# Where a batch's attention groups are cut into the matmul stream: two groups moved from one unit to the next

## The chip, the core and the metric

The kernel runs on one core of a Trainium2 chip. The metric is device time in microseconds (us) of one execution; the median of five runs is given. TensorE (PE) does the matmuls and its weight loads, VectorE (DVE) and ScalarE (ACT) move results out of the accumulation banks (PSUM) and do the elementwise work, GpSimd (POOL) and SyncE (SP) issue the transfers.

## What is computed

Linformer attention followed by a maxout layer. For each of 8 batches and 8 heads, with 1024 positions and head size 64:

```
k_proj = E @ k ;  v_proj = F @ v                  # 64 x 64 per head
attn   = softmax(q @ k_proj^T / 8)                # 1024 x 64
x      = attn @ v_proj                            # heads side by side: 8192 x 512
out    = max(x @ w1, x @ w2) @ w_out              # 512 -> 1024 -> 512
```

The kernel writes max(a, b) as relu(a - b) + b, so it needs x @ (w1 - w2) with a relu, and the product w2 @ w_out once.

## The kernel before

The main work is cut into 16 **units**, two for each batch: unit n handles one half of the positions of batch n // 2. A unit has a "down" part (the layer's second product, line 632, stored to the output) and an "up" part (the first product, line 554). Both are written as seven products in place of eight (a Strassen-like scheme), so there are sums of blocks on DVE (`step_s`, line 515), copies of partial results on ACT (`keep`, line 525) and adds on DVE (lines 569 and 656).

The order of the instructions is written by hand as a list of **slots**. Each down product of a unit is cut into pieces: two pieces of six matmuls in unit 0, three pieces of four in the others. A piece has the key `("P", unit, product, piece)`. In units 1 to 14 the up products of the next unit stand between the pieces, seven in each half, with keys `("U", unit, half, product)`; and in each half there is one empty slot `("G", unit, half)`. `at_slot(key, step, ...)` hangs further work behind a slot. All engines take their instructions in this order; each waits by semaphores for what it needs.

Attention of a batch consists of:

- `step_kv` (line 172): project k and v (16 matmuls of 512 columns into one bank), copied out by ACT (line 191) and DVE (lines 196, 200).
- the transposes: of the projected k (`step_kpt`, 16 small matmuls, or a transposing transfer on SP from batch 3 on), and of q (`step_qt`, matmuls copied out by DVE at line 242, for batches 0 and 1; `step_qt_dma`, two transposing transfers on SP, from batch 2 on).
- four **groups** (g, j): g picks four of the eight heads, j one half of the positions. A group has 16 score matmuls (line 266), exponentials on ACT, 8 matmuls for the sums (line 278), a logarithm and an exponential on ACT that invert them, 16 matmuls for the values (line 278 too), and products on DVE that write x (`xt_sb`). Unit 2n needs the two groups with j = 0 of batch n, unit 2n + 1 those with j = 1.

These small matmuls use a quarter or an eighth of the array each, and several run beside each other.

There are two forms of a group. The **loose** form (`step_sc`, `step_dn`, `step_inv`, `step_at`) hangs scores, sums, inversion and values at slots of their own. Its scores go to a pair of attention banks (`att_banks`, two pairs in turn as they come free), its values to two ordinary banks (`mm_bank`), and DVE multiplies each with a product of its own (line 325, two instructions of 512 columns). The **merged** form (`step_group`) puts the scores of one group and the sums and values of the group before it into one G slot; scores go to two ordinary banks with one exponential for each (line 351), sums and values to the two pairs of attention banks, the inversion is at lines 370 and 373, and one DVE product of 1024 columns (line 377) is issued at slot U 2 by `step_later`. In the batch's first group the scores stand behind the sums and values of the old group, in the others ahead of them.

Before the change, all four groups of batch 1 are in the loose form and hang at the pieces of unit 0, and the merged form begins with batch 2 in unit 1: its first scores at the second G slot. Batch 2's projection hangs at the first G slot of unit 1.

Transfers: POOL issues the loads of k, v and q (1 MB each). Batch 2's v and q are issued behind batch 1's projection. SP issues the stores of the output (256 KB each) and the transposing transfers in program order. The loads of batch 3 hang at `("U", 1, 0, 6)` behind `step_gate`, a POOL copy that waits for batch 2's transposed q.

Of the kernel before, what the change touches and what calls it, by code (L numbers as in the profile page):

```python
# [16 lines left out]
def kernel(  # L17
# [14 lines left out]
    B, H, S, D = q.shape  # L32
# [27 lines left out]
    def mm_bank(dtype=FP32, n=None):  # L60
        if n is None:
            n = turn.pop(0)
            turn.append(n)
        return ps.tile([128, 512 if dtype == FP32 else 1024], dtype, tag=f"mm{n}", name="mm_ps")

    def att_banks(dtype=FP32):
        return ps.tile(
            [128, 2, 512 if dtype == FP32 else 1024], dtype, tag="att", bufs=2, name="att_ps"
        )
# [6 lines left out]
            name=nc.get_next_instruction_name(),  # L76
# [30 lines left out]
    tiles = {b: {} for b in range(B)}  # L107
# [180 lines left out]
    def values_into(t, g, j, at_ps):  # L288
        for z in range(2):
            tiles_into(  # L290
                lambda o: at_ps[o][:, z * W : (z + 1) * W], t["ex", g, j],
                lambda rows, hh: t["vp"][rows, 4 * g + hh, z, :],
            )

    def new_xt(t):
        t["xt"] = xpool.tile([128, NP2, 2, HALF], FP16, tag="xt", name="xt_sb")

    def x_out(t, g, j):
        return t["xt"][:, 2 * g : 2 * g + 2, :, j * W : (j + 1) * W]
# [15 lines left out]
        ld = t["ld", g, j]  # L315
        nc.scalar.activation(out=ld, in_=ld, func=ACTF.Exp, scale=-1.0)

    def step_at(t, g, j):
        if "xt" not in t:
            new_xt(t)  # L320
        ld = t.pop(("ld", g, j))
        at_ps = [mm_bank() for _ in range(2)]
        values_into(t, g, j, at_ps)
        for o in range(2):
            nc.vector.tensor_tensor(  # L325
                out=x_out(t, g, j)[:, :, o, :],
                in0=at_ps[o].rearrange("q (z n) -> q z n", z=2),
                in1=ld[:, o, None, :].broadcast_to([128, 2, W]),
                op=ALU.mult,
            )  # L330
# [121 lines left out]
    U = {(b, o): {"n": n, "b": b, "o": o, "t": tiles[b]} for n, (b, o) in enumerate(units)}  # L452
# [260 lines left out]
    t = tiles[0]  # L713
# [25 lines left out]
    step_dn(t, 1, 0)  # L739
    step_inv(t, 1, 0)  # L740
    step_at(t, 0, 0)
    step_dn(t, 1, 1)
    step_inv(t, 0, 1)
    step_kv(t, 4, 8, "v")
    step_inv(t, 1, 1)
    step_at(t, 1, 0)
    step_wd(0)

# [7 lines left out]
    def loads(b, *names):  # L756
# [4 lines left out]

    slots = [
        (0, u0[0]), (None, f(step_at, 0, 1)), (1, u0[1]), (None, f(step_at, 1, 1)),
        (None, lambda: loads(1, "v", "q", "k")),
        (None, wd[1]), (2, u1[0]), (3, u1[1]), (4, u0[2]), (None, wt[0]), (5, u0[3]),
# [31 lines left out]
    def at_slot(key, s, *a):  # L797
        steps.setdefault(key, []).append(lambda: s(*a))
# [11 lines left out]
    t = tiles[1]  # L810
    at_slot((0, 19), new_attn, t)
    at_slot((0, 19), lambda: turn.__setitem__(slice(None), [2, 3]))
    for n, x in enumerate((
        "kv", "", "kpt", "qt00 qt10", "", "sc00 qt01 qt11", "sc10", "dn00 in00", "sc01",
        "at00 dn10 in10", "sc11", "at10 dn01 in01", "dn11 in11", "at01", "at11",
    )):
        key = ("P", 0, (n - 1) // 2, (n - 1) % 2) if n else (0, 19)
        for name in x.split():
            if name[0] == "k":
                if name == "kpt":  # L820
                    at_slot(key, step_kpt, t, 0, H, True)
                else:
                    at_slot(key, step_kv, t)
                    at_slot(key, loads, 2, "v", "q")
            else:
                g, j = int(name[2]), int(name[3])
                s_ = {"qt": step_qt, "sc": step_sc,
                      "dn": step_dn, "in": step_inv, "at": step_at}[name[:2]]
                at_slot(key, s_, t, *((4 * g, 4, 2 * j, 2 * j + 2) if name[:2] == "qt" else (g, j)))
        if n in (1, 5):  # L830
            at_slot(key, step_t, 1, (0, 1) if n == 1 else (2, 3))
        if 6 <= n < 10:
            at_slot(key, sums_x, U[0, 1], ((2, 0, 1, 3)[n - 6],))


    t = tiles[2]
    at_slot(("P", 0, 6, 0), new_attn, t)
    at_slot(("G", 1, 0), step_kv, t, 0, H, "kv", True)
    at_slot(("U", 1, 0, 1), step_kpt, t, 0, H, True)
    at_slot(("G", 1, 0), step_qt_dma, t, 0, H // 2)  # L840
    at_slot(("G", 1, 0), step_qt_dma, t, H // 2, H)
    at_slot(("U", 1, 0, 6), step_gate, t, "qt")
# [2 lines left out]
    for b in range(3, B):  # L845
        t = tiles[b]
        n = 2 * b - 3
# [3 lines left out]
        at_slot(("U", n, 0, 1), step_kv, t, 0, H, "kv", True, True)  # L851
        at_slot(("U", n, 0, 6), step_gate, t)
        at_slot(("U", n, 0, 6), loads, b + 1, "k", "v", "q")
    groups = [(tiles[b], g, j) for b in range(2, B) for j in range(2) for g in range(2)]
    none = (None, None, None)
    for i, (new, old) in enumerate(zip([*groups, none], [none, *groups])):
        n, h = divmod(i + 3, 2)
        if new[0] is not None:
            at_slot(("G", n, h), lambda t=new[0], h=h: t.__setitem__("first", (h, 1 - h)))
        at_slot(("G", n, h), step_group, *new, *old)  # L860
        at_slot(("U", n, h, 0), step_later)
        at_slot(("U", n, h, 2), step_later)
# [59 lines left out]
```

The softmax here doesn't subtract the row's maximum and nothing guards it: scores larger than these inputs give would overflow.

## Time and profile before

| | |
|---|---|
| median of 5 runs | 334.15 us (333.97 to 334.52) |
| the profiled execution | 333.97 us |
| its span, first to last instruction | 332.2 us |
| mean granted TensorE clock | 0.993 |
| PE busy | 320.1 us, 96% |
| DVE busy | 240.0 us, 72% |
| ACT busy | 201.6 us, 61% |
| chain that ended last | PE 86%, DMA 6%, DVE 4% |
| unit 0's pieces | 54.5 to about 71.5 us |
| unit 1's pieces and up products | about 71.5 to 91 us |

A matmul's record starts when it starts and its end is modelled, so records overlap; how long a stretch of matmuls really holds PE is read from the start of one to the start of the next that follows it. Busy shares are means over the whole span.

### The profile page before, as it was taken

The page shows a single profiled execution, that of the slowest core. Times are in us where ns is not written, and L with a number is a line of the kernel's source. Part 1 is how long each engine was busy: PE and PEld are TensorE (multiplying, and loading weights), DVE is VectorE, ACT ScalarE, POOL GpSimd, SP SyncE. Part 2 cuts the span into 40 slices and gives each one's busy share as a digit, 9 for nine tenths or more (in the row PEclk, how much of TensorE's full clock was granted, in tenths as well). Part 3 has the DMA queues.
Part 4 walks back from the last instruction along what each step waited for, and adds up shares of the span by engine and source line. Part 5 has one row for each costly group of instructions (what it writes and reads, how often), then busy time and mean ns, then how long its engine had stood idle before and what let it go on. Part 6 is the DMA issues. An engine that isn't in the chain of part 4 may idle for free.

```text
span 332.2 us, 9012 instructions
## 1 busy us (share of the span) xinstructions
PE 320.1 (96%) x3852; PEld 247.9 (75%) x3852; DVE 240.0 (72%) x426; ACT 201.6 (61%) x358; POOL 37.1 (11%) x56
## 2 busy tenths in 40 slices
PE   7976999999999999999999999999999999999994
PEld 3542546658788788878888788878887888888883
DVE  1345598997686779677969879677967796969572
ACT  1462522655677677767777577777776777764541
POOL 8546002003000030003000020003000000000000
PEclk9997999999999999999999999999999999999999
DMA  7999999997995969995999899997999321212132
GB/s 150 202 199 170 207 207 204 197 197 159 192 232 129 196 93 207 223 193 100 192 241 201 131 143 230 205 191 96 217 210 185 88 96 34 97 34 95 35 127 96
DMA packets 74680, 53.14 MB, mean 160 GB/s; under 512 B 29456, under 2 KB 74512, under 8 KB 74640
## 3 DMA queue, kind: packets, MB, share of 16 engines
q0 software_dynamic: 29376, 28.31, 54.3%
q1 hardware_dynamic: 45264, 24.25, 30.3%
q8 instruction: 30, 0.49, 0.6%
q14 instruction: 10, 0.08, 0.1%
HBM read 57.15 MB, written 16.78 MB: 223 GB/s over the span
## 4 chain that ended last, share of the span: by engine, by line
PE 86%; DMA 6%; DVE 4%; issue 1%; POOL 1%; ACT 1%; DVEq 0%; POOLq 0%
PE mm_ps L632 43%; PE mm_ps L554 25%; PE mm_ps L400 5%; PE att_ps L180 3%; DMA big<-in_moe_w_dram 3%; PE att_ps L278 3%; PE mm_ps L266 3%; DMA k_sb<-in_k_dram 3%; PE mm_ps L436 2%; DVE xt_sb L325 1%; DVE o_sb L656 1%; DVE gt_sb L569 1%; POOL k_sb L102 1%; PE mm_ps L237 1%; PE mm_ps L180 1%
## 5 line engine op out<-in xcount | busy, mean ns | idle before, releaser
L525 ACT COPY p_sb<-mm_ps 128x512 f32<-128x512 f32 x172 | 97.2, 593 | 46.8 <-PE mm_ps L554 33.2
L632 PEld LDWEIGHTS <-big 128*128 128x128 f16 x768 | 73.4, 98 | 12.3 <-issue 3.7
L632 PE MATMUL mm_ps<-T_sb,big 128*128 128x256 f16 x576 | 78.1, 273 | 0.0
L569 DVE TENSOR_TENSOR gt_sb<-mm_ps,p_sb 128x512 f16<-128x512 f32 x56 | 38.5, 688 | 46.5 <-PE mm_ps L554 46.5
L554 PE MATMUL mm_ps<-big,big 128*128 128x256 f16 x336 | 50.4, 273 | 0.0
L554 PEld LDWEIGHTS <-big 128*128 128x128 f16 x448 | 43.8, 98 | 5.2
L632 PEld LDWEIGHTS <-gt_sb 128*128 128x128 f16 x384 | 35.6, 98 | 10.1 <-issue 5.8
L632 PE MATMUL mm_ps<-wo_sb,gt_sb 128*128 128x256 f16 x256 | 42.9, 273 | 0.1
L554 PEld LDWEIGHTS <-wd_sb 128*128 128x128 f16 x336 | 32.9, 98 | 4.1 <-issue 0.3
L554 PE MATMUL mm_ps<-xt_sb,wd_sb 128*128 128x256 f16 x224 | 33.6, 273 | 0.2 <-ACT ex_sb L351 0.2
L351 ACT ACTIVATE ex_sb<-mm_ps 128x512 f16<-128x512 f32 x48 | 26.1, 596 | 9.2 <-PE att_ps L278 7.0
L656 DVE TENSOR_TENSOR o_sb<-mm_ps,p_sb 128x512 f32<-128x512 f32 x32 | 21.9, 685 | 10.7 <-PE mm_ps L632 7.2
L377 DVE TENSOR_TENSOR xt_sb<-att_ps,ld_sb 128x1024 f16<-128x1024 f32 x24 | 29.2, 1219 | 0.1
L632 PE MATMUL mm_ps<-m_sb,xt_sb 128*128 128x256 f16 x128 | 24.4, 273 | 0.0
L604 ACT ACTIVATE gt_sb<-mm_ps 128x512 f16<-128x512 f32 x28 | 16.8, 600 | 8.7 <-PE mm_ps L554 8.7
L515 DVE TENSOR_TENSOR big<-gt_sb 128x1024 f16<-128x1024 f16 x32 | 21.9, 684 | 0.2
L572 DVE TENSOR_SCALAR gt_sb<-gt_sb 128x512 f16<-128x512 f16 (+1 forms) x56 | 20.4, 364 | 1.9
L632 PE MATMUL mm_ps<-wo_sb,big 128*128 128x256 f16 x128 | 21.5, 273 | 0.0
L632 PE MATMUL mm_ps<-T_sb,gt_sb 128*128 128x256 f16 x128 | 21.5, 273 | 0.0
L632 PEld LDWEIGHTS <-xt_sb 128*128 128x128 f16 x192 | 18.8, 98 | 2.2
L229 POOL COPY junk<-kpt_sb 1x1 f16<-1x1 f16 x5 | 0.9, 178 | 166.4 <-DMA kpt_sb<-kp_sb 166.4
L400 PE MATMUL mm_ps<-xt_sb,wd_sb 128*128 128x512 f16 x64 | 16.3, 400 | 3.0 <-DVE wd_sb L414 2.1
(86 smaller groups left out, 435.4 us busy)
## 6 DMA issues: line engine op xcount, KB each, us to landing
out_dram<-o_sb SPq DMA_DIRECT2D x63, 256.0 KB, 2.7
k_sb<-in_k_dram POOLq DMA_DIRECT2D x7, 1024.0 KB, 10.6
v_sb<-in_v_dram POOLq DMA_DIRECT2D x7, 1024.0 KB, 17.3
q_sb<-in_q_dram POOLq DMA_DIRECT2D x7, 1024.0 KB, 22.3
k_sb<-in_k_dram POOLq DMA_DIRECT2D x4, 256.0 KB, 7.1
q_sb<-in_q_dram POOLq DMA_DIRECT2D x4, 256.0 KB, 8.3
v_sb<-in_v_dram POOLq DMA_DIRECT2D x2, 512.0 KB, 12.9
big<-in_moe_w_dram POOLq DMA_DIRECT2D x8, 128.0 KB, 10.7
```

Of the source, the lines that this page charges most:

```text
L180: nc.tensor.matmul(out=kv_ps[r * KP : (r + 1) * KP, 0:n], lhsT=eft[:, i, c, :], rhs=t[w][:, h0:h1, c, :], start=(c == 0), stop=(c == NC - 1),)
L351: nc.scalar.activation(out=t["ex", g, j][:, e, :], in_=banks[e], func=ACTF.Exp, scale=scale)
L377: nc.vector.tensor_tensor(out=x_out(t, g, j).rearrange("q z o n -> q o z n"), in0=at_ps.rearrange("q o (z n) -> q o z n", z=2), in1=ld[:, ...
L400: nc.tensor.matmul(out=h_ps, lhsT=wd_sb[:, r, fb * 128 : (fb + 1) * 128], rhs=t["xt"][:, r, :, j * W : (j + 1) * W], start=(r == 0), stop= ...
L515: nc.vector.tensor_tensor(out=S(i), in0=x, in1=y, op=op)
L525: copy(out=x, in_=bank)
L554: nc.tensor.matmul(out=bank[:, m * W : (m + 1) * W], lhsT=w_[:, n_, (2 * d + m) * 128 : (2 * d + m + 1) * 128], rhs=a[:, n_, :], start=(n ...
L569: nc.vector.tensor_tensor(out=c_blk(j, c), in0=two(x), in1=two(y), op=ALU.add)
L572: nc.vector.tensor_scalar_max(ap, ap, 0.0)
L604: nc.scalar.activation(out=out, in_=in_, func=ACTF.Relu)
L632: nc.tensor.matmul(out=bank[:, i * CH : (i + 1) * CH], lhsT=a(c)[:, i * 128 : (i + 1) * 128], rhs=w_(c), start=(n is not None and m == (lo ...
L656: nc.vector.tensor_tensor(out=o_sb, in0=two(x), in1=two(y), op=ALU.add)
```

## The change

Two of batch 1's four groups stay in unit 0, in the loose form, but gathered into three spots: both scores; both sums with their inversions; then the values of both together with the scores of the third group. The values of the second group go to a pair of attention banks (new argument `att` of `step_at`). The transposes of q for the second half of the positions get two slots of their own. The sums and values of the third group, and the whole fourth group, become merged groups at the two G slots of unit 1. So the list `groups` begins two groups earlier, and the pairs of new and old group are shifted. From unit 2 on the order is the same as before. Batch 2's projection goes from the first G slot of unit 1 to slot U 1 of that half, and its k transposes from U 1 to U 4.

```diff
-    def step_at(t, g, j):
+    def step_at(t, g, j, att=False):
         if "xt" not in t:
             new_xt(t)
         ld = t.pop(("ld", g, j))
-        at_ps = [mm_bank() for _ in range(2)]
+        if att:
+            both = att_banks()
+            at_ps = [both[:, o, :] for o in range(2)]
+        else:
+            at_ps = [mm_bank() for _ in range(2)]
         values_into(t, g, j, at_ps)
...
     for n, x in enumerate((
-        "kv", "", "kpt", "qt00 qt10", "", "sc00 qt01 qt11", "sc10", "dn00 in00", "sc01",
-        "at00 dn10 in10", "sc11", "at10 dn01 in01", "dn11 in11", "at01", "at11",
+        "kv", "", "kpt", "qt00 qt10", "", "sc00 sc10", "qt01", "qt11", "",
+        "dn00 in00 dn10 in10", "", "", "at00 AT10 sc01", "", "",
     )):
...
                 s_ = {"qt": step_qt, "sc": step_sc,
-                      "dn": step_dn, "in": step_inv, "at": step_at}[name[:2]]
-                at_slot(key, s_, t, *((4 * g, 4, 2 * j, 2 * j + 2) if name[:2] == "qt" else (g, j)))
+                      "dn": step_dn, "in": step_inv, "at": step_at, "AT": step_at}[name[:2]]
+                args = (4 * g, 4, 2 * j, 2 * j + 2) if name[:2] == "qt" else (g, j)
+                at_slot(key, s_, t, *args, *([True] if name[:2] == "AT" else []))
...
     t = tiles[2]
     at_slot(("P", 0, 6, 0), new_attn, t)
-    at_slot(("G", 1, 0), step_kv, t, 0, H, "kv", True)
-    at_slot(("U", 1, 0, 1), step_kpt, t, 0, H, True)
+    at_slot(("U", 1, 0, 1), step_kv, t, 0, H, "kv", True)
+    at_slot(("U", 1, 0, 4), step_kpt, t, 0, H, True)
     at_slot(("G", 1, 0), step_qt_dma, t, 0, H // 2)
     at_slot(("G", 1, 0), step_qt_dma, t, H // 2, H)
...
-    groups = [(tiles[b], g, j) for b in range(2, B) for j in range(2) for g in range(2)]
+    groups = [(tiles[b], g, j) for b in range(1, B) for j in range(2) for g in range(2)][2:]
     none = (None, None, None)
-    for i, (new, old) in enumerate(zip([*groups, none], [none, *groups])):
-        n, h = divmod(i + 3, 2)
+    for i, (new, old) in enumerate(zip([*groups[1:], none], groups)):
+        n, h = divmod(i + 2, 2)
```

## The prediction

> **What bounds the kernel now.** I read the page's busy lines and slices first, then PE's waits in the stretch that the change touches, then PE's timeline there, then the DVE, ACT and SP timelines beside it.
>
> ```profile
> PE 320.1 (96%) x3852; PEld 247.9 (75%) x3852; DVE 240.0 (72%) x426; ACT 201.6 (61%) x358; POOL 37.1 (11%) x56
> ...
> PE 7976999999999999999999999999999999999994
> ...
> PEclk9997999999999999999999999999999999999999
> ```
>
> From slice 6 (49.8 us) on PE is never under 90% busy, so from there time falls only if PE gets less to do or loses a gap. The waits view of PE between 52 and 110 us has two rows:
>
> ```profile
> PE mm_ps L278 <- DVE xt_sb L325: 0.6, 2, 0.3
> PE mm_ps L554 <- ACT ex_sb L351: 0.2, 1, 0.2
> ```
>
> That is little, but "busy" hides a second cost. The timeline of PE (start, duration, engine, line, tiles, count):
>
> ```profile
> 60.58 0.82 PE L632 MATMUL mm_ps<-T_sb,big 128*128 128x256 f16 x6
> 61.33 0.41 PE L266 MATMUL att_ps<-qt_sb,kpt_sb 64*32 64x256 f16 x16
> 61.67 0.83 PE L632 MATMUL mm_ps<-T_sb,big 128*128 128x256 f16 x6
> 62.43 0.30 PE L278 MATMUL att_ps<-ex_sb,ones 64*32 64x256 f16 x8
> 62.66 0.83 PE L632 MATMUL mm_ps<-T_sb,big 128*128 128x256 f16 x6
> ...
> 69.45 0.61 PE L632 MATMUL mm_ps<-T_sb,gt_sb 128*128 128x256 f16 x4
> 69.90 0.38 PE L632 MATMUL mm_ps<-T_sb,xt_sb 128*128 128x256 f16 x2
> 70.59 0.27 PE L278 MATMUL mm_ps<-ex_sb,vp_sb 64*32 64x256 f16 x1 [0.31 <-DVE xt_sb L325]
> 71.19 0.41 PE L278 MATMUL mm_ps<-ex_sb,vp_sb 64*32 64x256 f16 x15 [0.33 <-DVE xt_sb L325]
> 71.53 0.61 PE L632 MATMUL mm_ps<-wo_sb,gt_sb 128*128 128x256 f16 x4
> ```
>
> ```profile
> 82.37 1.04 PE L632 MATMUL mm_ps<-T_sb,big 128*128 128x256 f16 x8
> 83.33 0.41 PE L266 MATMUL mm_ps<-qt_sb,kpt_sb 64*32 64x256 f16 x16
> 83.68 0.61 PE L632 MATMUL mm_ps<-T_sb,big 128*128 128x256 f16 x4
> 84.47 0.60 PE L554 MATMUL mm_ps<-xt_sb,wd_sb 128*128 128x256 f16 x4 [0.18 <-ACT ex_sb L351]
> ...
> 90.79 0.38 PE L632 MATMUL mm_ps<-wo_sb,gt_sb 128*128 128x256 f16 x2
> 91.11 0.41 PE L266 MATMUL mm_ps<-qt_sb,kpt_sb 64*32 64x256 f16 x16
> 91.33 0.29 PE L278 MATMUL att_ps<-ex_sb,ones 64*32 64x256 f16 x8
> 91.44 0.40 PE L278 MATMUL att_ps<-ex_sb,vp_sb 64*32 64x256 f16 x16
> 91.78 0.39 PE L632 MATMUL mm_ps<-wo_sb,gt_sb 128*128 128x256 f16 x2
> ```
>
> Read starts, not durations. Six 128*128 matmuls take 0.66 (54.50 to 55.16, between two pieces with nothing between). From 60.58 to 61.67 is 1.09, so sixteen score matmuls in a spot of their own cost 0.43. Inside the merged spot at 91.11 the same sixteen take 0.22, eight sums 0.11, and the whole spot (scores, sums, values) 0.99 - 0.22 for its two big matmuls = **0.77**, where alone they would be 0.43 + 0.33 + 0.44 = 1.20. So each change from big to small matmuls and back costs about 0.21, whatever stands in the spot.
>
> **What the change moves, and its price on PE.** Work stays; spots go from eleven to five. Before, each spot by start differences less 0.66: scores 0.52 (58.49 to 59.67), 0.43, 0.48, 0.47; sums 0.33, 0.34; values and sums together 0.55 twice; values 0.44; the last values 1.42 (69.45 to 71.53). Sum 5.53. The last one holds a stall of 0.98: its two banks come free only as the two products L325 at 69.86 and 70.46 end, queued on DVE behind two adds L656 and six other L325. The eleventh spot, scores of batch 2 at 83.33, costs 1.31 - 0.87 = 0.44, and the next up product then waits for its bank's exponential: 84.47 instead of 84.12, 0.35. Total before: 5.53 + 0.44 + 0.35 = **6.32**.
>
> After, in order:
> - Both first scores in one spot: 0.52 + 0.22. The second needs the second transposed half of q, which DVE (L242, a pair that starts at 58.59 and ends at 59.87) has ready for PE at about 59.93, while PE arrives at 59.55: a new wait of 0.38. Queued behind it on PE is everything. Together **1.12**.
> - Both sums: 0.33 + 0.11 = **0.44**. Their exponentials (1.0 each on ACT) end near 61.8, PE comes near 63.9: hidden.
> - Values, values into an attention bank, scores: 0.44 + 0.22 + 0.22 = **0.88**. The banks' last readers are the two transposed copies and the two logarithms L312, all done by 66.0, PE comes at 66.3; the margin is thinnest here (0.3) for the second logarithm, which only the scores need, 0.4 later.
> - The first spot of unit 1, scores, sums, values: 0.77. Its values use the bank that the four products L325 read. These run behind two adds: PE's seventh product ends near 66.2, adds from 66.40, products from 67.60 at 0.60 each, the last over at 70.10. PE wants the bank at about 70.12, the release needs some 0.05: **0.81**. If DVE is late, PE pays one for one.
> - The second spot of unit 1 is a batch's first, where sums and values go ahead of the scores. The like spot in unit 3 (117.13 to 118.99, eight big matmuls out) takes 0.99, not 0.77. One piece later the up product waits for the exponential as it did before, 0.35: **1.34**.
>
> Total after: 1.12 + 0.44 + 0.88 + 0.81 + 1.34 = **4.59**. Difference 1.73.
>
> What else moves: the transposes of q are split over two slots; 128*128 transposes next to big matmuls cost no change (56.28 to 56.95 is 0.67 for six matmuls), so nothing. Batch 2's projection costs 72.20 to 74.80 less 0.66 = 1.94; in unit 3 it stands in the new slot and costs 110.37 to 112.75 less 0.44 = 1.94: nothing. Its k transposes cost 0.46 in either slot; they need the ACT copy L191 and the release of the projection's bank by DVE L196 (near 76.6 by DVE's rows from 75.3 on), PE comes at 77.7. The four L325 of 0.60 become two L377 of 1.22 on DVE, and two exponentials of 1.0 become four of 0.54: off PE's path while DVE has its gaps (15.14 busy of 20.24 between 71.60 and 91.84); without that cover 2.4 at most.
>
> SP keeps its order: four stores, then batch 2's two transposing transfers. They wait for q's landing (issued 55.73, 15.6 later, 71.3) and not for PE, and their first half lands 5.3 after issue, near 76.8; scores need it near 81.2. POOL's next loads hang on the second half, as before. Batch 3's q must land before 107.82 - 1.73 = 106.1; it landed at 103.1. Unit 2 and on have the same order as before, with PE full (35.85 per two units), so what is won by 85 us is kept to the end.
>
> **The rule that speaks against it.** Stores leave about 2 us earlier, while q is still coming in. The answer on the tiles of those transfers: that q took 15.6 from issue to landing, the one store that shared the time with it
>
> ```profile
> DMA to landing us min/median/max: 7.2/7.2/7.2
> ```
>
> where the next three took 2.7 to 4.0. Three stores of 256 KB at 205 GB/s (that stretch) are 3.8: q lands between 71.3 and 75.1, its first half by 80.5, in time by 0.7; batch 3's q by 106.9 at the latest, 0.8 late. I take nothing for it, and 0.8 as the far end. The Trainium skill, page "DMA: Bandwidth & Descriptors", section "Issuing engines are not separate DMA queues", says that transfers of all issuing engines share 16 DMA engines and interleave. By that rule alone the whole 3.8 would fall on q, the far end above; by the row of the three stores nothing would.
>
> **Sum.** The profiled execution took 333.97 with a span of 332.20; the median of the runs is 334.15. 333.97 - 1.73 = 332.24; with the 0.18 between profile and median, **332.4**. 0.2%, about what a measurement of this kernel can tell from no change, is 0.67.
>
> **Rivals.**
> - *The waits eat less.* Without the waits of 0.38, 0.35 and 0.22 it would be 331.45, the low end. Against: each has a row. Inside the forecast's own range.
> - *The transfers collide* (above), 0.8 to 1.2 lost in unit 3: 333.2 to 333.6. For: DMA engines are full until 70 us. Against: slack of 3.0 (106.1 - 103.1) for q and 0.5 for batch 3's transposed k (landed 117.90, scores 118.43).
> - *The saving does not come.* The 0.21 per spot could be a wait in disguise that reappears elsewhere: 333.5 to 334.8, no change. Against: it is equal in spots with different neighbours (0.33 and 0.34, 0.55 and 0.55).
> - *DVE becomes the bound in unit 1*, on the slower side: two L377 (2 x 1.22) and the projection's L196 and L200 (0.69 + 0.29) all stand in front of L569, which frees the bank of batch 2's scores. Uncovered they cost 3.42 - 1.73 = 1.7 above the median: 335.8. It decides from the point where L569 is over 1.2 late. Against: units 2 and on carry the same rows with DVE at 14 of 17.9 and PE full.
>
> **Chances.** Forecast (331.4 to 333.0) 0.75; collision 0.10; no saving 0.09; DVE bound 0.06. Range **331.4 to 333.5**: the forecast and nearly all of the collision. Faster 0.85, same 0.09, slower 0.06.
>
> **What would show it.** Right: between 58 and 85 us only three spots of small matmuls in unit 0; the pair of PE waits on L325 gone; a new wait of about 0.4 of PE L266 on DVE L242 near 59.6; the up product that started at 84.47 starts near 82.7; later units' pace unchanged. Wrong: PE waits on L377, L569 or L196 in unit 1; scores waiting on a transposing transfer; or the shift of 1.7 at 85 us not found at the end.

## The result, and the profile after

The changed kernel takes 331.71 us (median of 43 runs, 329.8 to 334.6) beside 333.75 us for the kernel before (80 runs, 331.3 to 337.3). The ratio is 0.9948, 95% interval 0.9937 to 0.9959: 1.74 us faster, 1.37 to 2.10 by the interval. The two medians by themselves differ by 2.04.

The profiled execution of after took 331.10 with a span of 329.3. Line numbers of after from 325 on are 4 higher than in the prediction, those from 829 on 5 (its L325 is now L329, L351 is L355, L373 is L377, L554 is L558, L569 is L573, L632 is L636). The page of after has

```profile
PE 318.2 (97%) x3852; PEld 248.4 (75%) x3852; DVE 239.7 (73%) x424; ACT 201.1 (61%) x359; POOL 36.9 (11%) x56
```

PE has the same 3852 matmuls and 1.9 us less busy time. Its waits between 52 and 110 us (engine, tile, line, what it waited for; total, times, longest):

```profile
PE att_ps L266 <- DVE qt_sb L242: 0.2, 1, 0.2
PE mm_ps L558 <- ACT ex_sb L355: 0.2, 1, 0.2
```

The two waits on the products of x are gone, the wait of the scores on DVE's copy of q is new, and the wait on the exponential has stayed. The waits view counts from the modelled end of the matmul before; by the starts below the first of the two is 0.38 (59.01 less 58.41, less the 0.22 of sixteen scores) and the second 0.35. PE's timeline of after (start, duration, line, tiles, count, idle time before it) shows the spots:

```profile
58.41 0.41 PE L266 MATMUL att_ps<-qt_sb,kpt_sb 64*32 64x256 f16 x16
59.01 0.41 PE L266 MATMUL att_ps<-qt_sb,kpt_sb 64*32 64x256 f16 x16 [0.18 <-DVE qt_sb L242]
59.35 0.83 PE L636 MATMUL mm_ps<-T_sb,big 128*128 128x256 f16 x6
...
65.07 0.38 PE L636 MATMUL mm_ps<-m_sb,big 128*128 128x256 f16 x2
65.38 0.41 PE L278 MATMUL mm_ps<-ex_sb,vp_sb 64*32 64x256 f16 x16
65.61 0.40 PE L278 MATMUL att_ps<-ex_sb,vp_sb 64*32 64x256 f16 x16
65.83 0.40 PE L266 MATMUL att_ps<-qt_sb,kpt_sb 64*32 64x256 f16 x16
66.16 0.61 PE L636 MATMUL mm_ps<-T_sb,gt_sb 128*128 128x256 f16 x4
...
81.42 0.60 PE L558 MATMUL mm_ps<-xt_sb,wd_sb 128*128 128x256 f16 x4 [0.18 <-ACT ex_sb L355]
...
82.94 0.38 PE L636 MATMUL mm_ps<-wo_sb,big 128*128 128x256 f16 x2
83.37 0.60 PE L558 MATMUL mm_ps<-big,big 128*128 128x256 f16 x4
```

In the third spot the starts tell the price: from 65.38 to 65.61 to 65.83 each set of sixteen small matmuls takes 0.22, and the one change into the spot and out of it is shared by all three.

For everything that follows, the **stage** is the time from the start of the first down matmul to the start of the 193rd (54.50 to 94.84 in before, 53.57 to 92.00 in after). It holds all that the change touches and leaves out what comes earlier and later. It is **40.35 us before and 38.43 after**, 1.92 less. From the 193rd to the last down matmul both profiles take 232.69: what was won is kept to the end. The profiled executions differ by 2.87 (333.97 against 331.10), but 0.92 of that is the earlier start at 53.57, ahead of everything that the change touches; it belongs to that execution.

### The profile page after: what moved, and what is told of

It reads as the page before. It is cut to its first block, busy times and chain, and to the rows that moved or that the text cites. A ratio compares the mean times of both kernels' runs of the same rounds, so it can differ in the third digit from the quotient of the medians.

```text
span 329.3 us, 9007 instructions
## 1 busy us (share of the span) xinstructions
PE 318.2 (97%) x3852; PEld 248.4 (75%) x3852; DVE 239.7 (73%) x424; ACT 201.1 (61%) x359; POOL 36.9 (11%) x56
## 4 chain that ended last, share of the span: by engine, by line
PE 86%; DMA 6%; DVE 4%; issue 1%; POOL 1%; ACT 1%; DVEq 0%; POOLq 0%
PE mm_ps L636 43%; PE mm_ps L558 25%; PE mm_ps L404 5%; PE att_ps L180 3%; DMA big<-in_moe_w_dram 3%; PE att_ps L278 3%; PE mm_ps L266 3%; DMA k_sb<-in_k_dram 2%; PE mm_ps L440 2%; DVE gt_sb L573 1%; POOL k_sb L102 1%; DVE o_sb L660 1%; PE mm_ps L180 1%; PE mm_ps L427 1%; DVE xt_sb L329 0%
## 5 line engine op out<-in xcount | busy, mean ns | idle before, releaser
L636 PEld LDWEIGHTS <-big 128*128 128x128 f16 x768 | 73.6, 98 | 12.0 <-issue 3.5
L636 PE MATMUL mm_ps<-T_sb,big 128*128 128x256 f16 x576 | 77.9, 273 | 0.0
L573 DVE TENSOR_TENSOR gt_sb<-mm_ps,p_sb 128x512 f16<-128x512 f32 x56 | 38.5, 688 | 45.7 <-PE mm_ps L558 42.6
L558 PE MATMUL mm_ps<-big,big 128*128 128x256 f16 x336 | 50.4, 273 | 0.0
L558 PEld LDWEIGHTS <-big 128*128 128x128 f16 x448 | 43.8, 98 | 5.3 <-issue 0.2
L636 PEld LDWEIGHTS <-gt_sb 128*128 128x128 f16 x384 | 35.7, 98 | 9.6 <-issue 5.4
L636 PE MATMUL mm_ps<-wo_sb,gt_sb 128*128 128x256 f16 x256 | 42.9, 273 | 0.1
L558 PEld LDWEIGHTS <-wd_sb 128*128 128x128 f16 x336 | 32.9, 98 | 4.2 <-issue 0.4
L558 PE MATMUL mm_ps<-xt_sb,wd_sb 128*128 128x256 f16 x224 | 33.6, 273 | 0.2 <-ACT ex_sb L355 0.2
L355 ACT ACTIVATE ex_sb<-mm_ps 128x512 f16<-128x512 f32 x50 | 27.2, 597 | 9.6 <-PE att_ps L278 7.0
L381 DVE TENSOR_TENSOR xt_sb<-att_ps,ld_sb 128x1024 f16<-128x1024 f32 x26 | 31.7, 1219 | 0.1
L636 PE MATMUL mm_ps<-m_sb,xt_sb 128*128 128x256 f16 x128 | 24.4, 273 | 0.0
L608 ACT ACTIVATE gt_sb<-mm_ps 128x512 f16<-128x512 f32 x28 | 16.8, 600 | 8.7 <-PE mm_ps L558 8.7
L636 PE MATMUL mm_ps<-T_sb,gt_sb 128*128 128x256 f16 x128 | 21.5, 273 | 0.0
L636 PE MATMUL mm_ps<-wo_sb,big 128*128 128x256 f16 x128 | 21.5, 273 | 0.0
L636 PEld LDWEIGHTS <-xt_sb 128*128 128x128 f16 x192 | 18.8, 98 | 2.2
```

The lines of the kernel that those rows point to most:

```text
L355: nc.scalar.activation(out=t["ex", g, j][:, e, :], in_=banks[e], func=ACTF.Exp, scale=scale)
L381: nc.vector.tensor_tensor(out=x_out(t, g, j).rearrange("q z o n -> q o z n"), in0=at_ps.rearrange("q o (z n) -> q o z n", z=2), in1=ld[:, ...
L558: nc.tensor.matmul(out=bank[:, m * W : (m + 1) * W], lhsT=w_[:, n_, (2 * d + m) * 128 : (2 * d + m + 1) * 128], rhs=a[:, n_, :], start=(n ...
L573: nc.vector.tensor_tensor(out=c_blk(j, c), in0=two(x), in1=two(y), op=ALU.add)
L608: nc.scalar.activation(out=out, in_=in_, func=ACTF.Relu)
L636: nc.tensor.matmul(out=bank[:, i * CH : (i + 1) * CH], lhsT=a(c)[:, i * 128 : (i + 1) * 128], rhs=w_(c), start=(n is not None and m == (lo ...
```

## Experiments

The stage is read from one profile of each kernel; it came out at 38.43 in both profiles of after and at 38.01 in both profiles of the kernel with later scores, so a few hundredths mean something in it. A single time does not: times of one kernel spread over 3 us and more.

**Do the two waits on L325 come from the banks?** The kernel before, with the last values of unit 0 in a pair of attention banks (`AT`; the new argument `att` of `step_at` comes in with it and is not shown):

```diff
-        "at00 dn10 in10", "sc11", "at10 dn01 in01", "dn11 in11", "at01", "at11",
+        "at00 dn10 in10", "sc11", "at10 dn01 in01", "dn11 in11", "at01", "AT11",
```

> The kernel before, with one edit: the last values of unit 0 go to a pair of attention banks, so that they need not wait for two DVE products. Stage: from the first down matmul to the first matmul of unit 2's fourth sum product (54.50 to 94.84 before, 40.34; 53.57 to 92.00 after, 38.43). Theory (price per spot plus the stall): only the stall of 0.98 goes, stage 39.3 to 39.5, the wait of 0.35 before the up product stays. Rival (the spots are free, the whole gain is waits): 38.4 to 38.6.

Measured: 39.37 instead of 40.35, and PE's waits between 45 and 110 us hold only the one on the exponential. The stall of 0.98 was a matter of where the last values go, and is worth all of its size: half of what the change gains.

**Does a spot have a price of its own?** After, with the second and third spot of unit 0 pulled apart again, so that unit 0 has six spots in place of three, all else the same:

```diff
-        "dn00 in00 dn10 in10", "", "", "at00 AT10 sc01", "", "",
+        "dn00 in00", "dn10 in10", "at00", "AT10", "sc01", "",
```

> The changed kernel with its second and third spot in unit 0 taken apart again: two sums and three of values, values, scores stand in five slots instead of two. Three more spots, no new wait. Theory: 3 x 0.21 = 0.63 more, stage 39.0 to 39.1. Rival (the price per spot is a wait in disguise and depends on the neighbours): 38.4 to 38.7.

Measured: 39.10, 0.67 more for three more spots, **0.22 each**, with the same two waits as after and no other. By the starts the two sums cost 0.33 each there and the values, values and scores 0.44, 0.45 and 0.44: each 0.22 more than inside a shared spot (0.11 and 0.22), whatever its neighbours. The price of a change between big and small matmuls is real and no wait in disguise.

**Are the two waits that after keeps worth what their starts say?** First the scores one slot later, so that DVE has the second half of q ready:

```diff
-        "kv", "", "kpt", "qt00 qt10", "", "sc00 sc10", "qt01", "qt11", "",
+        "kv", "", "kpt", "qt00 qt10", "", "", "sc00 sc10", "qt01", "qt11",
```

> The changed kernel with the first scores one slot later (and the two transposes behind them too), when DVE has copied both halves of q. Theory: the wait of 0.38 inside the first spot goes and nothing takes its place: stage 38.05, no PE wait on L242 in unit 0 left. Rival (another wait takes its place, in the later transposes or the sums): 38.4.

Measured: 38.01, 0.42 less, and the wait on L242 is gone. Then, with the scores back in their place, one piece of the down product from the first half of unit 1 to the second, between the scores and the up product that needs their bank (the expectations of the later runs with this edit name the halves the other way round):

```diff
-        for h, (x, y) in enumerate(((3, 3), (2, 1)) if n == 1 else ((2, 2), (2, 3))):
+        for h, (x, y) in enumerate(((3, 2), (2, 2)) if n == 1 else ((2, 2), (2, 3))):
```

> The changed kernel with one piece of unit 1 moved from before its first up product to behind its second spot of small matmuls. Theory: the up product finds its bank free (0.35 less), and its third product finds ACT's copy done (0.21 less): stage 37.85 to 38.1. Rival (the piece is missed in the first half, where the up product then waits for the first spot's exponentials): 38.4 or more.

Measured: 37.99, 0.44 less, the wait on L355 gone. That is more than the 0.35 at 81.42; the rest is a wait that the list of waits does not show, explained under the prediction below.

**Must the projection come later?** After, with it back in the first G slot, behind the first merged group:

```diff
-    at_slot(("U", 1, 0, 1), step_kv, t, 0, H, "kv", True)
-    at_slot(("U", 1, 0, 4), step_kpt, t, 0, H, True)
+    at_slot(("U", 1, 0, 1), step_kpt, t, 0, H, True)
...
         at_slot(("G", n, h), step_group, *new, *old)
+        if i == 0:
+            at_slot(("G", 1, 0), step_kv, tiles[2], 0, H, "kv", True)
```

> After, with only batch 2's projection moved back: it stands again in the first slot between units 0 and 1, right behind the first group of small matmuls, and its k transposes where the projection was (slot U 1). Theory (the later slots are needed because the projection shares the attention banks with the group, which sets them free only with its last logarithm): PE arrives at the projection with the pair still held and waits 1.4 to 1.5 us there, on ACT; from the first down matmul to the 193rd it takes 39.8 to 40.0 us instead of 38.43. Rival (the place of the projection is neutral, and only the number of spots counts): 38.3 to 38.5.

Measured: 39.92. The timeline of PE in this kernel:

```profile
69.51 0.41 PE L278 MATMUL att_ps<-ex_sb,vp_sb 64*32 64x256 f16 x16
71.39 0.38 PE L180 MATMUL att_ps<-k_sb,eft 128*64 128x512 f16 x1 [1.47 <-ACT ld_sb L374]
```

The projection goes into the pair of attention banks that the group's sums have just filled, and has to wait until ACT's logarithm has read them. Most of the change's gain (1.49 of 1.92) would be lost with this step left out: it belongs to the change.

**How much cover does DVE have in unit 1?** After, with four extra subtractions into a tile that nothing reads again, issued ahead of what the scores and sums of the second spot need (this leaves the computation as it is):

```diff
+    def more_dve(n):
+        dead = tiles[1]["kp"].rearrange("p h r d -> p (h r d)")
+        w_ = lambda r: wo_sb[0:KP, r : r + 2, :].rearrange("p r f -> p (r f)")
+        for _ in range(n):
+            nc.vector.tensor_tensor(out=dead, in0=w_(0), in1=w_(2), op=ALU.subtract)
+    at_slot(("U", 1, 0, 3), more_dve, 4)
```

> After, with four extra subtractions on DVE (into a tile that nothing reads again) in the first half of unit 1, ahead of the products that free the bank of batch 2's scores; about 2.7 us of DVE time. The test is how much cover DVE has there, which is the rival that the prediction called DVE bound. Theory (cover of 1.3 to 1.6 us): PE waits about 1.2 us on DVE, and the stage from the first to the 193rd down matmul takes 39.4 to 39.8 us instead of 38.43. Rival (DVE is already the bound in unit 1): the whole 2.7 shows, 41.1. If it shows nothing, 38.4 to 38.6, the cover is at least 2.7.

Measured: 39.59, 1.16 more. The four run from 77.56 to 80.32 on DVE, 2.76, so 1.6 us of DVE's time are covered. PE's timeline there, and the row of DVE's that matters:

```profile
80.78 0.41 PE L278 MATMUL att_ps<-ex_sb,vp_sb 64*32 64x256 f16 x16 [0.62 <-DVE kpt_sb L216]
81.00 0.79 PE L266 MATMUL mm_ps<-qt_sb,kpt_sb 64*32 64x256 f16 x16
...
80.65 0.67 DVE L573 TENSOR_TENSOR gt_sb<-mm_ps,p_sb 128x512 f16<-128x512 f32 x1
```

DVE is not the bound in unit 1, with 1.6 to spare at this place. What comes late first is the copy of the transposed k (L216), which frees an attention bank. But the sum is set by the product L573, which the prediction named: the sixteen scores, 0.40 long in after, take 0.79 here, since the third of them starts only at 81.38, 0.05 after L573 has ended. No row of the waits view lists this second wait.

**How late may batch 2's q be?** After, with its load held back behind an exponential, by a one-element copy on POOL; first behind the third group's:

```diff
-                    at_slot(key, loads, 2, "v", "q")
+                    at_slot(key, loads, 2, "v")
...
+        if n == 12:
+            def late(t=t):
+                nc.gpsimd.tensor_copy(out=junk, in_=t["ex", 0, 1][0:1, 0, 0:1])
+            at_slot(key, late)
+            at_slot(key, loads, 2, "q")
```

> After, with batch 2's load of q held back behind the third group's exponential: it is issued near 67.5 us instead of 54.8 and so shares its time with the stores of unit 0 more than in either kernel. The test is how much later q may land before it costs anything (the rival that the prediction called a collision). Theory (the scores of batch 2 have about 4 us of slack): q lands near 74.5, 2.9 later, its transposing transfers some 3 later, and the stage from the first to the 193rd down matmul stays at 38.4 to 38.5; at most 0.4 us is lost in unit 3, where batch 3's q follows. Collision rival: PE waits 0.8 us or more on a transposing transfer before the 193rd or in unit 3, and the kernel takes that much longer.

Measured: the stage 42.52, the time 335.02. The theory's landing time was wrong: q was issued at 67.14 and landed at 78.40, 11.3 later and not 7, since a load of 1 MB takes that long from its issue even with little ahead of it (batch 3's k, the first of its three loads, took 9.7 in after). Its transposed half landed at 82.95 beside 76.18 in after, past the slack of 4.1 (76.18 to the scores at 80.30). PE's timeline, and one row of the windows view (window, its length, then busy time and number of instructions of PE, PEld, DVE, ACT and POOL; the last three figures are the mean granted clock, the DMA share and GB/s):

```profile
83.00 0.63 PE L266 MATMUL mm_ps<-qt_sb,kpt_sb 64*32 64x256 f16 x16 [3.28 <-DMA qt_sb<-q_sb]
83.56 1.03 PE L636 MATMUL mm_ps<-T_sb,big 128*128 128x256 f16 x4
```

```profile
84.00:86.00 2.00, 2.00 (x11) 1.44 (x10) 0.00 (x0) 2.00 (x5) 0.14 (x1) 0.50 0.84 213
```

So q can come too late, and that costs more than the wait: after 3.28 us of idleness PE's clock fell to half, from 83.06 to about 86.5 (its mean is 0.76 over 82 to 84 and 0.88 over 86 to 88). From the scores to the up product `big,big` took 4.15 (83.00 to 87.15), where after needs 3.07 (80.30 to 83.37) with 0.35 and 0.21 of waiting in it: 1.64 us lost to the clock. The Trainium skill, page "TensorE: Matmul & The Clock Gate", section "Part 1: The HAM clock gate", says that about one idle window of 3.4 us brings half speed and a busy one of the same length full speed; the 3.4 at half speed here agrees, and the idle 3.28 is a little under the page's figure.

The same with a shorter delay, behind the second group's exponential (slot 9 and `t["ex", 1, 0]` in the edit above):

> The other side of the late q: batch 2's load of q held back behind the second group's exponential only, so issued near 61.4 us instead of 54.8. Theory (4.1 us of slack between the landing of the transposed half and its scores): q lands 1 to 3 later than the 71.6 of after, no wait of PE on a transposing transfer, the stage 38.4 to 38.5, the clock without a second stretch at half speed. Rival (any delay of q shows): PE waits 1 us or more at batch 2's scores.

Measured: q issued at 61.52, landed at 72.88, 1.3 later than in after; no wait on a transposing transfer and no second stretch at half speed. The slack holds. But the stage is 37.96, not 38.4: it became 0.47 **shorter**, and the wait on DVE's copy of q was gone, though nothing on PE or DVE had been moved. The timelines of the two kernels at that place show why. After:

```profile
54.80 0.88 POOL L102 DMA_DIRECT2D q_sb<-in_q_dram  x1
...
55.05 0.76 DVE L200 COPY vp_sb<-vp_sb 64x512 f16<-64x512 f16 x1
```

The kernel with q held back a little:

```profile
55.25 0.29 DVE L200 COPY vp_sb<-vp_sb 64x512 f16<-64x512 f16 x1
```

The same copy takes 0.29 without the issue of q's load beside it on POOL and 0.76 with it (it ends at 55.80, just after POOL is done at 55.68). All of DVE behind it is 0.47 late in after, and so is the copy L242 that PE waits for. The traffic was the same in both: 208 GB/s over the copy of 0.76 and 208 over that of 0.29.

**Is it the load's issue that holds DVE up?** After, with the load issued right behind that copy, by a one-element POOL copy that waits for it, and with the piece moved as above:

```diff
-                    at_slot(key, loads, 2, "v", "q")
+                    at_slot(key, loads, 2, "v")
+                    def behind_copy(t=t):
+                        nc.gpsimd.tensor_copy(out=junk, in_=t["vp"][0:1, 0, 0, 0:1])
+                    at_slot(key, behind_copy)
+                    at_slot(key, loads, 2, "q")
```

> After with two edits: batch 2's load of q is issued behind DVE's copy of the values (L200) instead of beside it, and one piece of the down product moves from the second half of unit 1 to the first, as in the kernel with that edit alone. The scores stay in their place. Question: why did the wait of PE on DVE's copy of q disappear when q's load was held back? Theory (the issue of the load on POOL, 0.88 us, holds up that copy, which took 0.76 us beside it and 0.29 us without): the copy takes 0.29, PE does not wait for L242, q is issued near 55.6 and lands within 1 us of before, and from the first to the 193rd down matmul it takes 37.5 to 37.7 us, 0.45 less from the one edit and 0.44 from the other than 38.43; the kernel then takes 330.4 to 331.0 us with before at 333.15 to 333.75. Rival (the wait went because q's data came in later, less traffic beside it): the copy stays near 0.76, PE waits 0.2 to 0.4 on L242, and the stage takes 38.0. If the two edits only move one wait, 38.0 as well.

Measured: the copy takes 0.29, the waits view lists no wait of PE in the stage, and the stage is 37.54. Its DVE and POOL timelines:

```profile
55.95 0.29 DVE L200 COPY vp_sb<-vp_sb 64x512 f16<-64x512 f16 x1
...
56.82 0.88 POOL L102 DMA_DIRECT2D q_sb<-in_q_dram  x1
```

q came in when it always had (14.4 us after its issue, at 71.17), so the rival that q's data came later falls. The median is 331.36 (11 runs), ratio 0.9926, interval 0.9898 to 0.9954, above the 330.4 to 331.0 expected; a part of the reason may be what the next runs show.

**Do the two small waits add up?** After with the later scores and the moved piece together, timed in the same rounds as after itself and as the kernel with later scores alone:

> After, with both of its small waits taken away: the two first scores stand one slot later (so that PE no longer waits for DVE's copy of the second half of q), and one piece of the down product moves from the second half of unit 1 to the first (so that PE no longer waits for ACT behind the last logarithm). Theory (two waits that add up, 0.4 and 0.4): from the first to the 193rd down matmul 37.55 to 37.75 us instead of 38.43, and the kernel 0.7 to 0.9 us faster than after, if the transposing transfer of k near 223 us lands 2.7 after its issue; with a late landing there (4.3, PE waits 1.0), which single kernels showed before, 0.2 slower to 0.1 faster than after. Rival (the two edits only move the same wait): 38.0 as with either alone.

> After unchanged, timed on the same chip and in the same rounds as the two below, to be compared with them: 1.6 to 1.9 us under the kernel before, 38.43 us from the first to the 193rd down matmul.

> The kernel with the two first scores one slot later, timed. By its stage (38.01 instead of 38.43) it would be 0.4 us faster than after; if the late landing of the transposing transfer of k near 223 us (PE waits 1.0) belongs to this kernel in every run, 0.6 slower; if it comes and goes, between the two.

| | stage | median | ratio to before, 95% interval |
|---|---|---|---|
| after | 38.43 | 332.04 (10 runs) | 0.9949 (0.9919 to 0.9980) |
| later scores | 38.01 | 331.34 (12) | 0.9937 (0.9912 to 0.9961) |
| both edits | 37.58 | 330.69 (6) | 0.9908 (0.9879 to 0.9937) |

They add up in the stage: 0.85 for 0.42 and 0.44, and the waits view lists none for PE from 50 us to the end. It is the fastest kernel of the study by its median, 1.35 under after, but 0.85 is all that the stage accounts for, and the intervals overlap.

What blurs the times is a wait far behind the change. The first profile of later scores has it in PE's timeline:

```profile
223.31 0.41 PE L266 MATMUL mm_ps<-qt_sb,kpt_sb 64*32 64x256 f16 x16 [1.03 <-DMA kpt_sb<-kp_sb]
```

The transposing transfer of batch 6's k, 2.7 us from issue to landing in the others, took 4.3 there. From the 193rd to the last down matmul that execution took 233.70, and others with the late transfer 233.57 to 233.83, not 232.69. It does not belong to a kernel: the second profile of later scores was without it, the second of after had it (4.3, 233.63), and it was there in 7 of the study's 14 profiled executions, the one with the load behind the copy among them, where it made 0.9 of that execution's 332.12; whether it stood behind that kernel's median is not shown. Neither of the two profiles with the old cut (before, and before with the free banks) had it; two are too few to say that the change brought it on. All other transposing transfers of k on SP in these executions took 2.6 to 2.8. Why that one is late in some executions stays open.

## Why the prediction was right, point by point

Predicted 332.4, range 331.4 to 333.5; measured 331.71. Of the 0.69 between, 0.40 lies in the base (334.15 by five runs, 333.75 by eighty) and 0.19 in the stage (1.92 won, 1.73 forecast); the rest is within what the medians blur. The mechanism was the forecast's. By its own steps:

| step | predicted | measured in after | from the starts |
|---|---|---|---|
| both scores, with the wait on L242 | 1.12 | 1.12 | 57.57 to 59.35, less 0.66 |
| both sums | 0.44 | 0.44 | 61.56 to 63.31, less 1.31 |
| values, values, scores | 0.88 | 0.87 | 64.63 to 66.16, less 0.66 |
| first spot of unit 1 | 0.81 | 0.77 | 68.14 to 69.57, less 0.66 |
| second spot of unit 1 | 0.99 | **0.77** | 78.99 to 80.63, less 0.87 |
| up product's wait behind it | 0.35 | 0.35 | 81.07 to 81.42 |
| sum | 4.59 | 4.32 | |

Two terms were mis-sized and nearly cancel, which is luck:

- *The second spot of unit 1* was priced by the like spot of unit 3, at 0.99. In unit 3 PE pauses 0.22 between the second and the third of the sixteen score matmuls (in the records of after 115.59 and 115.81); in unit 1 they run through. The pause is a wait on DVE that no row of the waits view lists:

```profile
115.59 0.62 PE L266 MATMUL mm_ps<-qt_sb,kpt_sb 64*32 64x256 f16 x16
...
115.07 0.68 DVE L573 TENSOR_TENSOR gt_sb<-mm_ps,p_sb 128x512 f16<-128x512 f32 x1
```

  The third score matmul is the first into the second bank of the scores, the bank that L573 reads last. L573 ends at 115.75, the matmul starts at 115.81; in before it is 118.60 and 118.65. The first scores of batches 4 to 7 show the same pause and the same 0.05 in both kernels. In unit 1 L573 ends at 79.08, 1.2 ahead of the scores. So the 0.99 held a wait of its own place, and was no price of the order in the spot. With 0.77 the sum is 4.32 and the gain 2.0. At the up product before and after are 2.13 apart (84.47 less 81.42 less the earlier start of 0.92); 0.10 of the difference is a wait in before that the forecast's sum did not hold, at the product at 79.31 (four big matmuls from 78.77 would end at 79.21).
- *A missed term of 0.21.* Of those 2.13 the stage keeps 1.92. The product at 83.37 should have started at 83.15 (82.94 and two big matmuls, 0.22). ACT's timeline of after:

```profile
81.74 0.60 ACT L374 ACTIVATE ld_sb<-att_ps 128x512 f32<-128x512 f32 x1
82.22 1.09 ACT L529 COPY p_sb<-mm_ps 128x512 f32<-128x512 f32 x2
```

  The logarithm L374 of the merged group is new at this place and stands ahead of the two copies that free the banks of the up products; the second ends at 83.31, and PE waits for it. The prediction counted ACT's added instructions as off PE's path, and did not ask what stands behind the logarithm on ACT. The run with the piece moved got the 0.35 back and about half of this, 0.44 in all: there the third product still starts 0.10 late (83.53, where two big matmuls from 83.21 would end at 83.43), just after the second copy (ended 83.49).

The term for before's stall (0.98) was right (39.37 with it alone taken out), and so was 0.21 per spot (0.22 measured). The projection at 1.94 and its k transposes at 0.46 cost what was said: in after 71.76 to 74.14 less 0.44 and 0.46. That its move costs nothing was right too, but half of the story: its old place would have cost 1.49.

The new wait of 0.38 was of the right size for a reason that the prediction did not see. It took DVE's row of before as it was; that row was late because the load's issue, at 55.73 in before, held up a copy ahead of it, and the wait need not have been there:

```profile
55.97 0.75 DVE L200 COPY vp_sb<-vp_sb 64x512 f16<-64x512 f16 x1
```

The rivals:

- *The transfers collide.* The mechanism set in for the stores, the price did not come. The three stores took 5.1 to 5.8 us from issue to landing (before 2.7 to 4.0), as the tile's answer in after says:

```profile
DMA to landing us min/median/max: 5.1/5.7/5.8
```

  and q 16.8 instead of 15.6. But the second profile of after has the stores at 4.7 to 4.8 and q at 15.4, so only the stores' delay belongs to the change. In the first profile q's transposing transfers were issued at 71.71 (before 71.42) and their first half landed 4.1 us ahead of its scores. Batch 3's q landed at 102.99, before 103.1. The bound of 3.8 on q's delay was far too wide: 1.2 and nothing were measured. The stores gave way, not the load.
- *The saving does not come*: excluded by the price per spot and by 232.69 in both profiles behind the stage.
- *DVE becomes the bound*: not so, with 1.6 us of cover in the end. The point of "over 1.2 late" was right: L573 ends at 79.08 in after, and the third score matmul, which needs its bank 0.05 later, starts at 80.30. The argument that units 2 and on carry the same rows with PE full was not: there PE pauses for this very product.

## What to carry to other kernels

On a PE that is never idle, what can still be won is the changes between full-size and small matmuls, about 0.2 us each, and waits of a few tenths that "busy" hides; gather small matmuls into few spots, and price them by differences of starts, which also show waits that a list of waits leaves out (here 0.22 at the first scores of each batch from batch 3 on, still there in after). When a step moves, ask on every engine what is queued behind each instruction that moves with it (here a logarithm ahead of two copies), and ask of a late row what made it late before taking it as given. A transfer that is late by less than its slack costs nothing; once past it PE pays for the wait, and after a long one (3.28 us here; not after the 1.47 of the projection) for the slow clock behind it.

## What the runs showed of the hardware that was not expected

- The issue of a load on POOL (0.88 us) holds up a DVE copy from on-chip memory to on-chip memory in fp16: 0.76 us beside it, 0.29 without. Elementwise sums of two operands in on-chip memory were not held up: two L515 in before that began inside an issue (79.82 to 80.69) took 0.41 and 0.68, at 79.84 and 80.17, as everywhere. The Trainium skill, page "SBUF — State Buffer", section "Who interferes with whom", has the rule: GpSimd and VectorE share one pair of ports, a copy in a fast mode takes it for the whole instruction, and whoever comes second waits. The copy's rows agree.
- After 3.28 us without work PE ran at half clock for 3.4 us, at a price of 1.64 us on top of the wait.
- A 1 MB load took 9.3 to 11.4 us from issue to landing even when little stood ahead of it (each batch's k from batch 3 on in before and after, and the two late loads of q); the 7 us between two loads' landings is no measure of it.
- One transposing transfer of the same size and place took 2.7 or 4.3 us (4.2 to 4.5 where it was late, over all kernels) from one execution to the next of the same kernel, 1.0 us of PE's time; the cause is not known.
